# Second FFN: stores on GpSimd's queue, raw tokens loaded half a pass earlier, one operand's split moved, six staging tiles at the end

## The chip, the cores and the metric

One core of a Trainium2 chip runs the whole program as one launch. The metric is the device time of the launch in microseconds (us), the median of several runs. Before the change it is 1320.53 us over three runs (1319.96 to 1321.88).

## The reference

```python
attn_out = attention between x [8,8,512,64] and state [8,8,32,64], rows of x and of state concatenated
x = attn_out.transpose(0, 2, 1, 3).reshape(B * S, H * D)      # 4352 used rows x 512 (8 * (512 + 32))
x = ((x @ w1) * (x @ w2)) @ w3 @ w_out                          # first FFN, d_ff 1024
gate = 1.0 / (1.0 + np.exp(-(x @ w_gate)))                      # second FFN, d_ff 1536
return (gate * (x @ w_val) @ w_out2).astype(np.float32)
```

The change lies in the second FFN alone: gate, value, product and down projection for 34 blocks of 128 tokens, and the stores of its result.

## The kernel before

**Order of the whole.** Attention and the first FFN run first and leave their result `y` in DRAM (`y_d`). The second FFN starts at about 540 us in the profiled execution. Each matrix product there is cut as Strassen-Winograd does it (seven products of half-size blocks, `OPS`, `SEQ`, `DOWN`), and each operand is split into a high and a low part (`split`, `operand`, `part`), so that one product is three matmuls per 128 rows of the contraction.

**Loops.** The tokens are cut into five pairs of chunks, `blocks = [8, 8, 6, 6, 6]` (line 239), so a matmul streams n = 512 columns in the first two and 384 in the last three. For each chunk `c` there are three passes `g` over a third of the hidden columns (`steps`, line 1591). One pass is `gate_val(c, g, 0, between)`, 14 steps, and `gate_val(c, g, 1, ...)`, 14 steps; three steps into the first half `between` runs `down` of the pass before, 7 products of 2 steps. A step is 6 matmuls.

**The order of the work.** It is written out by hand. `begin` counts the steps (`clock["now"]`) and runs what is due; `later(k, cost, fn)` makes `fn` due `k` steps on; `fill` puts token work into steps where VectorE has credit. PE, ACT, DVE, POOL and SP each execute in the order in which instructions were emitted.

**Weights.** `Stream` (lines 1245 to 1264) holds 16 tiles `wt` (256 KB each, one per step of `gate_val`) and 4 tiles `wo` (512 KB each, one per product of `down`). A tile's next load is issued on SP's queue when the tile has been used. With four `wo` tiles, the load issued after product s is needed by product s + 4.

**Stores.** After the last pass of a chunk, `store` (line 1478) is due for each of its blocks every three steps: VectorE transposes the block in 32x32 pieces into one of three `sv` tiles, and two steps later `out_` issues four DMAs of 64 KB on SP's queue (line 1486). The three `sv` tiles also hold copies of partial sums in `evict` (lines 1530 and 1538). The last chunk is stored by `last_store` (line 1493): TensorE transposes a block into a PSUM bank, ACT or DVE copies it into an `sv` tile, and one DMA of 256 KB stores it, on SP's queue for even and ACT's for odd blocks. All six of its blocks follow the last product (lines 1576 to 1580). Two of these six blocks (32 and 33, the second and third in order) are rows of `state`: their destination has the dimensions 4 by 32 by 512, the others 128 by 512.

**Tokens.** `next_tokens(c + 1, at)` (line 1268) issues the four raw loads of the next chunk on SP's queue (`y_raw`, line 1117), and lists eight differences (`diff`) and fourteen splits (`part`). Each split has a step count after `half[i]`, the middle of a pass. The call is at the start of a chunk's last pass (lines 1616 to 1620).

**Operands of the down projection.** `operand(s, jj)` (line 1336): ACT copies the high part, one step later VectorE makes the low part. Operands 0 to 3 are put into the schedule by `have` (line 1358), operands 4 to 6 by `down` itself (line 1575), four products ahead.

Of the kernel before, what the change touches and what calls it, by code (L numbers as in the profile page):

```python
# [8 lines left out]
F32 = mybir.dt.float32  # L9
# [108 lines left out]
def tile_state_attention__then__gated_ffns(  # L118
# [19 lines left out]
    nc = tc.nc  # L138
    P = 128
    B, H, S, D = x.shape  # L140
    NS = state.shape[2]
    DM, DFF = w1.shape
# [6 lines left out]
    KM = DM // P  # L149
# [87 lines left out]
    NPAIR = 5  # L237
# [6 lines left out]
    NPASS = 3  # L244
# [18 lines left out]
    with tc.manual_schedule(engines={mybir.EngineType.PE}):  # L263

        at = tc.alloc_tile_pool(name="at", bufs=1, reuse_waits="tile")
# [830 lines left out]
        todo = []  # L1096
# [104 lines left out]
        ps2 = tc.alloc_tile_pool(name="ps2", bufs=1, space=PSUM, reuse_waits="tile")  # L1201
        tc.swap_default_side()
        c2 = tc.alloc_tile_pool(name="c2", bufs=1, reuse_waits="tile")
# [6 lines left out]
        clock = {"now": 0, "us": 0.0, "vector": 0.0, "load": 0.0}  # L1210
        due = {}
        tokens = []
        half = {}
        ready = {(0, o, kb) for o in range(7) for kb in range(2)}

        def later(k, cost, fn):
            due.setdefault(clock["now"] + k, []).append((cost, fn))
# [140 lines left out]
        def have(q, jj, cc, n):  # L1358

            cost = n / 840  # L1360
            if q == 0:
                if (jj, cc) == (1, 0):
                    for i in range(2):
                        later(2 + i, 0.0, lambda i=i: operand(0, i))
                        later(3 + i, cost, lambda i=i: first_sum(i, n))
                        later(5 + i, 0.0, lambda i=i: operand(1, i))
                return
            if cc:
                later(3, cost, lambda: minus(tv[jj], pv[1, jj, 1], tv[jj]))
                later(6, cost, lambda: minus(pv[0, jj, 1], pv[1, jj, 1], pv[0, jj, 1]))  # L1370
                if jj == 0:
                    for i in range(2):
                        later(4 + i, 0.0, lambda i=i: operand(2, i))
                        later(6 + i, 0.0, lambda i=i: operand(3, i))
            elif jj:
                for i in range(2):
                    later(5 + i, cost, lambda i=i: minus(tv[i], pv[1, i, 0], tv[i]))
# [100 lines left out]
        def store(c, cc, m):  # L1478
            t = c2.tile([P, 4, KM, 32], F32, name="sv", bufs=3)
            for d in range(KM):  # L1480
                nc.vector.transpose(out=t[:, :, d], in_=acc[d, cc][:, m * P : (m + 1) * P])

            def out_():
                dst = rows(c, cc, m)
                for i in range(4):
                    nc.sync.dma_start(
                        out=dst[:, :, i * P : (i + 1) * P],
                        in_=t[32 * i : 32 * i + 32].rearrange("t j d e -> t j (d e)"),
                    )

            later(2, 0.0, out_)

        def last_store(c, cc, m, i):
            pt = ps2.tile([P, DM], F32, tag="A", name="pot", bufs=2)
            for d in range(KM):
                nc.tensor.transpose(pt[:, d * P : (d + 1) * P], acc[d, cc][:, m * P : (m + 1) * P], unit)
            t = c2.tile([P, 4, KM, 32], F32, name="sv", bufs=3)
            copy("dve" if i % 2 else "act", t, pt.rearrange("p (c i d) -> p i c d", c=KM, i=4))
            blk = first[c] + (cc * blocks[c] // 2) + m
            if blk < B * SC:  # L1500
                b, r = order[blk // SC], blk % SC
                dst = out[b * ROWS : b * ROWS + S].rearrange("(p c) e -> c p e", c=SC)[r]
            else:
                b = 4 * (blk - B * SC)
                dst = out.rearrange("(b r) e -> b r e", b=B)[b : b + 4, S:]
            (nc.scalar if i % 2 else nc.sync).dma_start(out=dst, in_=t.rearrange("p i c d -> p (i c d)"))

        def down(c, g, tail=False):
            n = blocks[c] * P // 2
            banks = {}  # L1510

            def more(o, d, cc):
                nc.vector.tensor_tensor(out=acc[d, cc], in0=o, in1=acc[d, cc], op=ALU.add)  # L1513
                vector(n / 840)

            def also(v, d, cc):
                nc.vector.tensor_tensor(out=acc[d, cc], in0=v, in1=acc[d, cc], op=ALU.add)

            def new_acc(d, cc):
                acc[d, cc] = c2.tile([P, NB], F32, name=f"acc{d}{cc}")[:, :n]  # L1520
                return acc[d, cc]

            def evict(k, d, o):
                if k == 1:
                    if g == 0:
                        s = new_acc(d, 0)
                        copy("act", s, o)
                        later(1, n / 1600, lambda: nc.vector.tensor_copy(out=new_acc(2 + d, 0), in_=s))
                    else:
                        s = c2.tile([P, NB], F32, name="sv", bufs=3)[:, :n]  # L1530
                        copy("act", s, o)
                        later(1, n / 840, lambda: also(s, d, 0))
                        later(2, n / 840, lambda: also(s, 2 + d, 0))
                elif k == 5:
                    if g == 0:
                        copy("act", new_acc(2 + d, 1), o)
                    else:
                        s = c2.tile([P, NB], F32, name="sv", bufs=3)[:, :n]
                        copy("act", s, o)
                        later(2, n / 840, lambda: also(s, 2 + d, 1))  # L1540
                elif k == 6:
                    if g == 0:
                        copy("act", new_acc(d, 1), o)
                    else:
                        more(o, d, 1)
                else:
                    e = {3: (d, 1), 7: (2 + d, 1), 2: (d, 0), 4: (2 + d, 0)}[k]
                    more(o, *e)

            for s, k in enumerate(DOWN):  # L1550
                w = wos.next()
                for d in range(2):
                    begin(1.36 * n / 512)
                    if k in (1, 6, 2):
                        tag, bufs = ("B", 2) if k == 6 else ("o", 3)
                        banks[k, d] = ps2.tile([P, 512], F32, tag=tag, name=f"po{k}", bufs=bufs)[:, :n]
                    o = banks[{5: 1, 3: 1, 7: 6, 4: 6}.get(k, k), d]
                    for jj in range(2):
                        x = parts[s, jj]
                        for i, h in ((0, 0), (0, 1), (1, 0)):  # L1560
                            nc.tensor.matmul(  # L1561
                                o,
                                w[:, jj, i, d * P : (d + 1) * P],
                                x[h],
                                start=k in (1, 6, 2) and jj == 0 and i + h == 0,
                                stop=jj == 1 and i == 1,
                                skip_group_check=True,
                            )
                    fill()
                    evict(k, d, o)  # L1570
                wos.load()
                for jj in range(2):
                    del parts[s, jj]
                    if s + AHEAD < len(DOWN):
                        later(1 + jj, 0.0, lambda s=s, jj=jj: operand(s + AHEAD, jj))
            if g == NPASS - 1:
                todo = [(cc, m) for cc in (1, 0) for m in range(n // P)]
                for i, (cc, m) in enumerate(todo):
                    if tail:
                        last_store(c, cc, m, i)  # L1580
                    else:
                        later(2 + 3 * i, 1.0, lambda cc=cc, m=m: store(c, cc, m))

        names = [(f"p{q}{jj}{cc}", 1, NB) for q in range(2) for jj in range(2) for cc in range(2)]
        names += [(f"acc{d}{cc}", 1, NB) for d in range(KM) for cc in range(2)]
# [27 lines left out]
        }  # L1613
        with tc.manual_schedule(engines=ordered):
            for i, (c, g) in enumerate(steps):
                if g == NPASS - 1 and c + 1 < NPAIR:
                    def at(k, i=i):
                        return lambda: i in half and clock["now"] > half[i] + k

                    tokens += next_tokens(c + 1, at)  # L1620

                def between():
                    if i:
                        down(*steps[i - 1])

                gate_val(c, g, 0, between)
                half[i] = clock["now"]
                gate_val(c, g, 1, lambda: None)
            for _ in range(3):
                begin(0.0)  # L1630
            down(*steps[-1], tail=True)
            while due:
                begin(0.0)
# [31 lines left out]
```

## Time and profile before

| what | value |
|---|---|
| median of 3 runs | 1320.53 us (1319.96 to 1321.88) |
| the profiled execution's own time | 1318.98 us |
| its span, first to last instruction | 1317.2 us |
| PE busy | 1277.9 us (97%) |
| DVE busy | 950.4 us (72%) |
| ACT busy | 672.3 us (51%) |
| POOL busy | 24.9 us (2%) |
| DMA, mean rate over the span | 238 GB/s |

The span is what the trace covers; 1.8 us of the execution's own time lie around it. A busy PE counts the modelled ends of pipelined matmuls. In the chain of waits 84% of the span is PE and 6% DMA.

### The profile page before, as it was taken

The page shows a single profiled execution, that of the slowest core. Times are in us where ns is not written, and L with a number is a line of the kernel's source. Part 1 is how long each engine was busy: PE and PEld are TensorE (multiplying, and loading weights), DVE is VectorE, ACT ScalarE, POOL GpSimd, SP SyncE. Part 2 cuts the span into 40 slices and gives each one's busy share as a digit, 9 for nine tenths or more (in the row PEclk, how much of TensorE's full clock was granted, in tenths as well). Part 3 has the DMA queues.
Part 4 walks back from the last instruction along what each step waited for, and adds up shares of the span by engine and source line. Part 5 has one row for each costly group of instructions (what it writes and reads, how often), then busy time and mean ns, then how long its engine had stood idle before and what let it go on. Part 6 is the DMA issues. An engine that isn't in the chain of part 4 may idle for free.

```text
span 1317.2 us, 21517 instructions
## 1 busy us (share of the span) xinstructions
PE 1277.9 (97%) x7816; PEld 1103.7 (84%) x7816; DVE 950.4 (72%) x1839; ACT 672.3 (51%) x1307; POOL 24.9 (2%) x50
## 2 busy tenths in 40 slices
PE   7999999999999999999999999999899999999995
PEld 5487778878778789888888888889899999999994
DVE  6893889797797856265868857697377757786755
ACT  6993757667577555252354435344235334444432
POOL 0000000000000000000000000000000000000000
PEclk9999999999999999999999999999899999999998
DMA  9994597886987732676776967669788898889743
GB/s 309 351 274 137 184 306 243 297 295 252 330 268 286 281 114 73 206 252 203 251 200 192 253 195 237 201 188 269 246 264 251 245 288 287 253 237 294 245 146 96
DMA packets 181666, 312.86 MB, mean 238 GB/s; under 512 B 45368, under 2 KB 77624, under 8 KB 174648
## 3 DMA queue, kind: packets, MB, share of 16 engines
q1 hardware_dynamic: 169076, 264.43, 63.7%
q0 software_dynamic: 5760, 37.23, 7.8%
q10 hardware_dynamic: 6724, 9.83, 2.2%
q8 instruction: 62, 1.02, 0.3%
q14 instruction: 44, 0.36, 0.1%
HBM read 256.38 MB, written 55.05 MB: 236 GB/s over the span
## 4 chain that ended last, share of the span: by engine, by line
PE 84%; DMA 6%; DVE 5%; ACT 3%; issue 1%; SPq 0%; DVEq 0%; ACTq 0%
PE psA L1392 20%; PE po L1561 16%; PE psB L1392 10%; PE pab L225 9%; PE py L225 8%; PE psC L1392 5%; PE pab L228 4%; PE py L228 4%; DMA wo<-wod 3%; PE pwp L225 2%; PE psw L533 2%; DMA wq<-w12d 2%; PE pwp L228 1%; PE pxt L290 1%; DVE y L1123 1%; DMA out<-sv 1%
## 5 line engine op out<-in xcount | busy, mean ns | idle before, releaser
L1392 PE MATMUL psA<-y,wt 128*128 128x384 f32 (+1 forms) x1440 | 299.8, 356 | 0.0
L1392 PEld LDWEIGHTS psA<-y,wt 128*128 128x128 f32 x1440 | 258.9, 188 | 22.5
L1561 PE MATMUL po<-ph,wo 128*128 128x384 f32 (+1 forms) x1260 | 256.0, 362 | 14.6 <-DMA wo<-wod 11.2
L1561 PEld LDWEIGHTS po<-ph,wo 128*128 128x128 f32 x1260 | 229.5, 191 | 38.7 <-issue 8.3
L158 ACT ACTIVATE u<-psA 128x384 f32<-128x384 f32 (+1 forms) x120 | 64.0, 533 | 239.3 <-PE psA L1392 227.0
L1392 PE MATMUL psB<-y,wt 128*128 128x384 f32 (+1 forms) x720 | 159.5, 356 | 0.0
L1392 PEld LDWEIGHTS psB<-y,wt 128*128 128x128 f32 x720 | 130.0, 188 | 11.2
L225 PE MATMUL py<-u,wp 128*128 128x512 f32 (+1 forms) x576 | 131.8, 381 | 0.0
L225 PEld LDWEIGHTS py<-u,wp 128*128 128x128 f32 x576 | 102.8, 188 | 27.2 <-issue 7.9
L225 PE MATMUL pab<-aT,sw 128*128 128x512 f32 x448 | 122.1, 394 | 0.8 <-DVE aT L163 0.8
L1513 DVE TENSOR_TENSOR acc<-po,acc 128x384 f32<-128x384 f32 (+1 forms) x140 | 83.7, 607 | 37.3 <-PE po L1561 36.7
L225 PEld LDWEIGHTS pab<-aT,sw 128*128 128x128 f32 x448 | 82.6, 188 | 17.6 <-DVE aT L163 1.1
L1419 DVE TENSOR_TENSOR p<-psB,u 128x384 f32<-128x384 f32 (+1 forms) x60 | 36.6, 610 | 80.5 <-ACT u L158 72.9
L1421 ACT ACTIVATE p<-p 128x384 f32<-128x384 f32 (+1 forms) x90 | 50.6, 563 | 77.1 <-DVE p L1419 77.1
L1123 DVE TENSOR_TENSOR ph<-p,ph 128x384 fp32r<-128x384 f32 (+1 forms) x120 | 72.5, 605 | 10.4 <-ACT ph L158 10.4
L1392 PE MATMUL psC<-y,wt 128*128 128x384 f32 (+1 forms) x360 | 79.8, 356 | 0.0
L1392 PEld LDWEIGHTS psC<-y,wt 128*128 128x128 f32 x360 | 65.0, 188 | 5.6
L228 PE MATMUL pab<-aT,sw 128*128 128x512 f32 x224 | 69.1, 390 | 0.0
L228 PE MATMUL py<-u,wp 128*128 128x512 f32 (+1 forms) x288 | 67.7, 377 | 0.0
L158 ACT ACTIVATE ph<-p 128x384 fp32r<-128x384 f32 (+1 forms) x120 | 64.7, 561 | 0.0
L158 ACT ACTIVATE ph<-t 128x384 fp32r<-128x384 f32 (+1 forms) x90 | 49.6, 563 | 28.0 <-DVE t L1123 26.6
L1123 DVE TENSOR_TENSOR ph<-t,ph 128x384 fp32r<-128x384 f32 (+1 forms) x90 | 54.1, 604 | 10.8 <-ACT ph L158 10.8
(145 smaller groups left out, 1801.2 us busy)
## 6 DMA issues: line engine op xcount, KB each, us to landing
wt<-wd SPq DMA_DIRECT2D x420, 256.0 KB, 3.2
wo<-wod SPq DMA_DIRECT2D x105, 512.0 KB, 4.0
wq<-w12d SPq DMA_DIRECT2D x32, 1024.0 KB, 8.7
raw<-in_moe_w SPq DMA_DIRECT2D x32, 512.0 KB, 6.1
wd<-wstb POOLq DMA_DIRECT2D x12, 1024.0 KB, 5.4
raw<-in_moe_w_out SPq DMA_DIRECT2D x20, 512.0 KB, 5.6
wd<-wsta POOLq DMA_DIRECT2D x12, 768.0 KB, 4.2
xn<-in_x SPq DMA_DIRECT2D x56, 128.0 KB, 6.5
```

The costliest lines, as they stand in the source:

```text
L158: return nc.scalar.activation(out=o, in_=i, func=AF.Copy)
L225: nc.tensor.matmul(o, w[i], xx[k], start=begin and n == 0 and i + k == 0, stop=False)
L228: nc.tensor.matmul(o, w[1 - late], xx[late], start=False, stop=end and n == len(pairs) - 1)
L290: nc.tensor.transpose(pt[:, c * P : (c + 1) * P], xn[b][:, g, c].rearrange("p a d -> p (a d)"), ident,)
L533: nc.tensor.matmul(pts[k][NS * g : NS * g + NS, a * WQ : (a + 1) * WQ], stT[64 * k : 64 * k + 64, g, self.b * NS : (self.b + 1) * NS], w[6 ...
L1123: nc.vector.tensor_tensor(out=o, in0=x0, in1=x1, op=ALU.subtract)
L1392: nc.tensor.matmul(o, w[:, i, kb * P : (kb + 1) * P], xx[kb][h], start=start, stop=i == 1 and kb == 1, skip_group_check=True,)
L1419: nc.vector.tensor_tensor(out=t, in0=o, in1=kept[a, what], op=ALU.add)
L1421: later(2, 0.0, lambda: nc.scalar.activation(out=t, in_=t, func=AF.Sigmoid))
L1513: nc.vector.tensor_tensor(out=acc[d, cc], in0=o, in1=acc[d, cc], op=ALU.add)
L1561: nc.tensor.matmul(o, w[:, jj, i, d * P : (d + 1) * P], x[h], start=k in (1, 6, 2) and jj == 0 and i + h == 0, stop=jj == 1 and i == 1, sk ...
```

## The change

Operand 3 of the down projection is split three steps later. The stores of the first four chunks are issued by GpSimd's queue and not by SP's. In the last chunk the six stored blocks are staged in the six `yt` tiles (tag `m`) and not in the three `sv` tiles, every third PSUM bank is of tag `C`, and the three blocks of the second half are transposed and stored one product earlier (after product 2, the sixth of the seven, before product 4). The next chunk's tokens are begun in the middle of the second pass instead of at the start of the third; the step counts of their splits still refer to the middle of the third.

```diff
-                        later(6 + i, 0.0, lambda i=i: operand(3, i))
+                        later(9 + i, 0.0, lambda i=i: operand(3, i))
...
                 for i in range(4):
-                    nc.sync.dma_start(
+                    nc.gpsimd.dma_start(
                         out=dst[:, :, i * P : (i + 1) * P],
...
-            pt = ps2.tile([P, DM], F32, tag="A", name="pot", bufs=2)
+            tag, bufs = ("C", 1) if i % 3 == 2 else ("A", 2)
+            pt = ps2.tile([P, DM], F32, tag=tag, name="pot", bufs=bufs)
...
-            t = c2.tile([P, 4, KM, 32], F32, name="sv", bufs=3)
+            t = c2.tile([P, 4, KM, 32], F32, tag="m", name="yt", bufs=6)
...
-            if g == NPASS - 1:
-                todo = [(cc, m) for cc in (1, 0) for m in range(n // P)]
-                for i, (cc, m) in enumerate(todo):
-                    if tail:
-                        last_store(c, cc, m, i)
-                    else:
-                        later(2 + 3 * i, 1.0, lambda cc=cc, m=m: store(c, cc, m))
+                if tail and k in (2, 4):
+                    for m in range(n // P):
+                        last_store(c, int(k == 2), m, (k == 4) * n // P + m)
+            if g == NPASS - 1 and not tail:
+                for i in range(2 * n // P):
+                    cc, m = 1 - i // (n // P), i % (n // P)
+                    later(2 + 3 * i, 1.0, lambda cc=cc, m=m: store(c, cc, m))
...
-                if g == NPASS - 1 and c + 1 < NPAIR:
-                    def at(k, i=i):
-                        return lambda: i in half and clock["now"] > half[i] + k
-
-                    tokens += next_tokens(c + 1, at)
-
...
                 half[i] = clock["now"]
+                if g == NPASS - 2 and c + 1 < NPAIR:
+                    def at(k, i=i + 1):
+                        return lambda: i in half and clock["now"] > half[i] + k
+
+                    tokens += next_tokens(c + 1, at)
                 gate_val(c, g, 1, lambda: None)
```

## Rows read from the trace of the kernel before

**Rows 1.** Groups by line: engine, operation, shapes, count | busy us, mean ns | idle us, releasers.

```profile
L1561 PE MATMUL po<-ph,wo 128*128 128x384 f32 (+1 forms) x1260 | 256.0, 362 | 14.6 <-DMA wo<-wod 11.2 <-ACT sv L158 3.4
```

**Rows 2.** Timeline of PE: start, us, what, [idle before it, and its releaser].

```profile
929.94 9.30 PE L1561 MATMUL po<-ph,wo 128*128 128x384 f32 x36 [5.23 <-DMA wo<-wod]
...
979.01 8.07 PE L1561 MATMUL po<-ph,wo 128*128 128x384 f32 x36 [2.32 <-DMA wo<-wod]
...
1116.73 6.48 PE L1561 MATMUL po<-ph,wo 128*128 128x384 f32 x36 [1.44 <-DMA wo<-wod]
```

**Rows 3.** Chain of waits in order of time: start, us, what.

```profile
916.38 6.26 PE po L1561 x36
923.26 6.54 DMA wo<-wod
...
968.36 2.09 PE po L1561 x12
970.47 8.40 DMA wo<-wod
```

**Rows 4.** Timeline of SP's queue: start, us, issues.

```profile
905.39 1.37 SPq L1260 DMA_DIRECT2D wt<-wd  x3
907.17 1.76 SPq L1486 DMA_DIRECT2D out<-sv  x4
909.03 1.36 SPq L1260 DMA_DIRECT2D wt<-wd  x3
...
965.68 2.49 SPq L1117 DMA_DIRECT2D yf<-yd  x4
```

**Rows 5.** DMA issues by line: KB each, median us to landing.

```profile
wo<-wod SPq DMA_DIRECT2D x105, 512.0 KB, 4.0
```

**Rows 6.** Windows: us, busy of each engine, granted clock of PE, DMA share, GB/s.

```profile
930.00:939.00 9.00, 9.00 (x36) 9.00 (x37) 2.79 (x5) 0.00 (x0) 0.00 (x0) 0.66 0.48 152
...
953.00:965.00 12.00, 12.00 (x71) 12.00 (x70) 6.79 (x14) 5.22 (x12) 0.00 (x0) 1.00 0.80 251
...
972.00:980.00 8.00, 5.68 (x33) 5.39 (x33) 7.15 (x16) 2.79 (x7) 0.00 (x0) 1.00 1.05 385
980.00:990.00 10.00, 10.00 (x50) 10.00 (x49) 6.70 (x13) 0.98 (x2) 0.00 (x0) 0.83 0.58 167
```

**Rows 7.** DMA issues on POOL, from the views of lines 662 and 1089: ns min/median/max.

```profile
L662 POOL DMA_DIRECT2D w12d<-wq x4: 533/602/1096, 21.9 to 47.9; - x4
...
L1089 POOL DMA_DIRECT2D wd<-wsta x12: 531/531/540, 156.9 to 420.5; - x12
```

**Rows 8.** Timeline of ACT, DVE and PE from 1015 to 1022 us.

```profile
1017.86 0.93 ACT L158 ACTIVATE ph<-p 128x384 fp32r<-128x384 f32 x2
...
1019.22 1.34 PE L1561 MATMUL po<-ph,wo 128*128 128x384 f32 x6 [0.95 <-ACT sv L158]
...
1019.86 0.53 ACT L1421 ACTIVATE p<-p 128x384 f32<-128x384 f32 x1 [0.69 <-DVE p L1419]
```

**Rows 9.** Timeline of all engines from 1295 us to the end.

```profile
1296.09 1.94 DVE L1513 TENSOR_TENSOR acc<-po,acc 128x384 f32<-128x384 f32 x4
...
1299.21 1.03 PE L1496 MATMUL pot<-unit,acc 128*128 128x128 f32 x8
1299.41 0.56 DVE L1513 TENSOR_TENSOR acc<-po,acc 128x384 f32<-128x384 f32 x1 [0.48 <-PE po L1561]
...
1301.01 1.15 ACTq L1506 DMA_DIRECT2D out<-sv  x1
...
1312.90 0.69 DVE L159 COPY sv<-pot 128x512 f32<-128x512 f32 x1 [9.54 <-DMA out<-sv]
1313.63 0.35 ACTq L1506 DMA_DIRECT2D out<-sv  x1
```

**Rows 10.** Windows of half a us in the last stores (columns as in rows 6).

```profile
1301.50:1302.00 0.50, 0.19 (x2) 0.00 (x0) 0.00 (x0) 0.00 (x0) 0.00 (x0) 1.00 1.02 385
...
1307.50:1308.00 0.50, 0.00 (x0) 0.00 (x0) 0.00 (x0) 0.42 (x1) 0.00 (x0) 0.50 0.31 70
```

## The prediction

> **What bounds the kernel now.** I read the views from coarse to fine. The table of the profile shows PE busy for 97% of the span, so what can be had is PE's idle time and slow time, not the work of another engine. The groups by line say where PE idles in the second FFN: its down projection waits 11.2 us for `wo` tiles and 3.4 us for ACT's copies into `sv` [rows 1]. PE's timeline places the `wo` waits: five, the longest 5.23 us at 929.94, then 2.32 at 979.01 and 1.44 at 1116.73, the other two sharing what is left, 2.2 us [rows 1, 2]. All lie in chunks with n = 384.
>
> The chain of waits in order of time says that they have two causes [rows 3]. At 916.38 a `down` begins. Its first product is two steps, and 12 matmuls take 2.09 us, so the first new `wo` load is due at 918.47. It is issued at 923.26, 4.8 us late, and lands 6.5 us later. SP's queue shows why it is late: before it, three `wt` loads and four stores alternate, and one such group takes 909.03 - 905.39 = 3.64 us [rows 4], while PE needs three `wt` tiles every 3 x 1.045 = 3.13 us. Each stored block thus puts SP back by 0.5 us. At 970.47, in contrast, the load is issued on time (968.36 + 2.09) but takes 8.40 us to land where the median is 4.0 [rows 3, 5]: four raw loads of tokens were issued at 965.68, just in front of it [rows 4], and the DMA engines are full, at a share of 1.05 and 385 GB/s [rows 6]. The wait at 1116.73 is the same collision one chunk on; the two unshown ones follow stores, as the first does.
>
> Two stalls cost a second time: TensorE's granted clock is 0.66 in 930 to 939 and 0.83 in 980 to 990 [rows 6], the stretches behind them. Part of each runs at 1.2 instead of 2.4 GHz.
>
> Last comes the end. The final matmul is done at about 1299.2, the last store is issued at 1313.63, and the span ends at 1317.2 [rows 9]: 18 us in which PE does only transposes. DVE's last copy starts at 1312.90 after an idle 9.54 us: it waited for a staging tile that an earlier store still held.
>
> **The change part by part**, against the profiled execution (1318.98 us, 1.55 us below the median; gains are carried over to the median unchanged).
>
> *Stores on POOL's queue.* SP loses 112 issues. Between two blocks it is left with three `wt` loads, 1.4 us per 3.13 us [rows 4], so it waits for PE and the `wo` load goes out when due: 918.47 + the 6.54 us it took [rows 3] is 925.0, and product 4 needs it at 916.38 + 8.4 = 924.7. By the median, 4.0, it is well in time. So the waits after stores go: 11.2 - 2.32 - 1.44 = 7.4 us, and the slow clock at 930, 9 x (1 - 0.66) = 3.0 us. On POOL nothing else is queued in this phase. The 40 DMAs that it issues earlier take 0.53 to 1.10 us each [rows 7]; four at 0.53 are 2.1 us per block, inside 3.13. The store's bytes stay on the DMA engines, so I leave 1 us of new waiting for them. **Gain 9.4**, bounds 0 (the stores delay weights wherever they are issued) and 10.4.
>
> The Trainium skill speaks against this part: DMA: Bandwidth & Descriptors, Rules for kernel authors, says that spreading DMAs over issuing engines does not help, since all run on the same 16 DMA engines, and saves only issue time. By it the gain here would be 0 (the first rival below) if issue time were not the bound; that SP's groups take 3.64 us against 3.13 is the row that says it is.
>
> *Raw loads half a pass sooner.* The four loads (384 KB each at n = 384) now meet 14 + 3 steps, 17.8 us, of `wt` loads with 16 tiles ahead before the next `down`. Beside the 251 GB/s that PE eats (256 KB per 1.045 us), 385 GB/s leave 134, so 1.57 MB are made up for in 11.7 us. SP meets four more issues there, 2.5 us [rows 4], covered by the 16 tiles. So 2.32 + 1.44 us go, and 10 x (1 - 0.83) = 1.7 us of slow clock. **Gain 5.5**, bounds 0 and 5.5. The eight differences on DVE go along into the second half of the pass, where DVE has room (6.79 us busy of 12 in 953 to 965 [rows 6]; the eight are 4.5 us at 0.56), and raw and `yt` tiles are held longer, which nobody waits for; no gain and no cost.
>
> *Operand 3.* Its two ACT copies (0.93 us at 1017.86) stand before the copy into `sv` for which PE idles 0.95 us at 1019.22 [rows 8]; behind it, PE starts earlier. But the second `sv` copy stands behind a sigmoid at 1019.86 that waits for DVE, and that order stays: what is saved at the first wait is paid at the second. Its two low parts on DVE move behind four additions, to about the time when product 3 reads them. Forecast **0**; bounds: all 3.4 us of `sv` waits gained, or one DVE operation late, 0.56 us [rows 9], in each of 15 `down`, 8 us lost.
>
> *The end.* Twelve of the 24 transposes move before the last 12 matmuls: 1.03 us per 8 [rows 9], 1.55 us, only shifted. They need additions that DVE works off at 1296.09 to 1298.03, the second of them by about 1297.1, when product 2 ends: no wait, at most 0.5 us. The other twelve wait for the last addition (1299.41 + 0.56 is 0.8 us after the last matmul). With a staging tile for each block, the last issue is bounded by 1299.2 + 1.55 + 0.8 + 1.55 of transposes + two copies (0.69, 0.60) + ACT's own issue of up to 1.15 us in front of its copy [rows 9], 1305.5 instead of 1313.63: 8.1 us gained if the transfers keep up. They may not. Blocks 32 and 33 move at 70 GB/s and a share of 0.31 where a plain block moves at 385 and 1.02 [rows 10], as if on a quarter of the engines. From the second store's issue, 1301.01, to the landing that frees the last copy, 1312.90, are 11.9 us. In the new order that store can go at about 1298.7 (DVE's 1298.03 + a copy); + 11.9 + 0.7 for a sixth block at 385 GB/s + 2 of finishing is 1313.3, a gain of 3.9, and 3 if the late transposes cost what they can. I take 5.5, between the two, nearer the transfers: **gain 5.5**, bounds 3 and 8.
>
> Sum: 9.4 + 5.5 + 0 + 5.5 = 20.4. 1320.5 - 20.4 = **1300.1**; I say 1300.
>
> **Rivals.**
>
> *The DMA engines, not SP's issue, are what the stores fill.* Then loads are as late as before after stores, and only the raw loads' waits and the end go: 5.5 + 5.5 = 11, 1309.5. For it: shares near 1 around the waits [rows 6]. Against it: the 923.26 load was issued late, not only slow. Chance 0.17.
>
> *POOL is too slow, and the kernel gets slower.* The three `sv` tiles are the place: if four issues on POOL take longer than 3.13 us (0.78 each), each block puts POOL back, DVE's transposes wait for a tile, and every DVE operation behind them waits, then PE. At the slowest POOL issue on record, 1.10 [rows 7], 20 blocks at n = 384 lose 4.4 - 3.13 and 8 at n = 512 (3.13 x 512 / 384 = 4.17 us per three steps) 0.23: 27 us, against 20.4 gained: 1327. It decides from about 1.0 us per issue on. Against it: the median is 0.53, for DMAs of the same 128 rows. Chance 0.05. The Trainium skill, SBUF — State Buffer, section SBUF: two separate sides, names such a mechanism: descriptors of DMAs issued from GpSimd cannot be written while VectorE runs a copy in a two-port mode, and it gives some 3.1 us instead of 0.62. By that figure, on every issue, it would be some 250 us lost; no row of this trace shows it.
>
> *Operand 3 comes late in every `down`:* 8 us lost of 20.4, 1308. Chance 0.08.
>
> *The raw loads only move their collision* into the second half-pass and still leave `wo` late: 5.5 less, 1305.6. Chance 0.08.
>
> **How the numbers follow.** The forecast has the remaining 0.62, and its own bounds reach from 1320.5 - 10.4 - 5.5 - 3.4 - 8 = 1293 to about 1306. The range reaches over the faster rivals, 1293 to 1310. 0.2% (2.6 us) is about what a measurement of this kernel can tell from no change. All cases but POOL's lie 10 us or more below the time before; I leave 0.02 in between for two of them together. Faster 0.92, same 0.03, slower 0.05.
>
> **What would show it.** Stores on POOL's queue at about 0.5 us each and no `DMA wo` among PE's releasers after them; `wo` landings near 4 us after the third pass begins; a granted clock of 1.0 from 925 on; the `sv` waits still there, not larger; the last store issued near 1305 and the span ending 4 to 6 us after it. Wrong would be: `wo` loads issued on time but landing in 6 us or more (first rival), DVE's transposes waiting for stores (second), PE waiting for `ph` in product 3 (third).

## The result, and the profile after

The change makes the kernel faster by what was forecast: 21.0 us were gained where 20.4 had been summed up.

| what | before | after |
|---|---|---|
| median of 4 runs | 1320.24 us | 1299.26 us (1298.55 to 1300.80) |
| ratio | 1 | 0.9845, 95% interval 0.9826 to 0.9863 |
| the profiled execution's own time | 1318.98 us | 1299.36 us |
| its span | 1317.2 us | 1296.9 us |
| PE idle in the down projection | 14.6 us | 5.4 us |
| mean granted clock of TensorE | 0.990 | 0.997 |

The groups by line of the kernel after (columns as in [rows 1]; the down projection's line is now 1562) show where PE's time came from, and where the stores went:

```profile
L1562 PE MATMUL po<-ph,wo 128*128 128x384 f32 (+1 forms) x1260 | 251.6, 357 | 5.4 <-ACT sv L158 2.8
...
L1486 POOL DMA_DIRECT2D out<-sv x112 | 61.6, 550 | 599.9 <-DVE sv L1481 593.5
```

`DMA wo`, 11.2 us in [rows 1], is no longer among PE's releasers. The waits view of the kernel after (engine, what waits, for whom: us in total, times, longest) says what the 5.4 us are:

```profile
PE po L1562 <- ACT sv L158: 2.8, 5, 1.1
PE po L1562 <- DVE ph L1123: 2.3, 4, 0.8
```

The waits for `sv` are a little smaller than the 3.4 us before. The waits for `ph`, the parts of the split operands, are new; [rows 1] have none. The chain of waits in order of time, around the `down` that began at 916.38 in [rows 3], holds no DMA any more; its 84 matmuls run through:

```profile
915.26 2.08 PE psA L1392 x12
917.35 1.04 PE psC L1392 x6
918.38 14.56 PE po L1562 x84
```

SP's queue in the same stretch (columns as in [rows 4]) has no stores between the weights, and the first new `wo` load goes out at 920.50, which is 918.38 plus the two steps of the first product; it was 4.8 us late before:

```profile
890.34 28.40 SPq L1260 DMA_DIRECT2D wt<-wd  x28
920.50 12.84 SPq L1260 DMA_DIRECT2D wo<-wod  x7
```

In the windows that answer to [rows 6] (same columns) the granted clock is 1.00, behind the first store wait as behind the third pass; before, 0.66 and 0.83 were granted there, a part of the time at 1.2 instead of 2.4 GHz:

```profile
930.00:940.00 10.00, 10.00 (x59) 10.00 (x59) 3.25 (x7) 2.38 (x5) 0.00 (x0) 1.00 0.88 279
...
975.00:985.00 10.00, 10.00 (x60) 10.00 (x59) 3.45 (x7) 2.87 (x6) 0.00 (x0) 1.00 0.88 282
```

The end is shorter too. In the timeline of all engines of the kernel after, product 2 ends at 1283.31, where the transposes that were moved begin; before, it ended at 1297.13 (the transposes' start of 1299.21 [rows 9] less the 2.08 us of the last product):

```profile
1283.31 1.47 PE L1497 MATMUL pot<-unit,acc 128*128 128x128 f32 x12
...
1285.11 1.15 ACTq L1507 DMA_DIRECT2D out<-yt  x1
...
1287.52 1.20 PE L1497 MATMUL pot<-unit,acc 128*128 128x128 f32 x9 [0.32 <-DVE acc L1514]
...
1289.49 0.34 ACTq L1507 DMA_DIRECT2D out<-yt  x1
```

**Where the 20.3 us of the span went.** `wo` waits 11.2; slow clock 3.0 + 1.7 = 4.7 (the prediction's terms from [rows 6]); from the end of product 2 to the end of the span 1317.2 - 1297.13 = 20.1 before and 1296.9 - 1283.31 = 13.6 after, 6.5 less; `sv` waits 0.6 less; `ph` waits 2.3 more. That is 20.7.

### The profile page after: what moved, and what is told of

Read it like the earlier page. It is cut to its first block, busy times and chain, and to the rows that moved or that the text cites. A ratio compares the mean times of both kernels' runs of the same rounds, so it can differ in the third digit from the quotient of the medians.

```text
span 1296.9 us, 21521 instructions
## 1 busy us (share of the span) xinstructions
PE 1273.8 (98%) x7816; PEld 1100.1 (85%) x7816; DVE 951.6 (73%) x1839; ACT 668.8 (52%) x1307; POOL 86.7 (7%) x162
## 4 chain that ended last, share of the span: by engine, by line
PE 86%; DVE 8%; ACT 3%; DMA 1%; issue 1%; ACTq 0%; SPq 0%; DVEq 0%
PE psA L1392 20%; PE po L1562 16%; PE psB L1392 10%; PE pab L225 9%; PE py L225 9%; PE pab L228 5%; PE psC L1392 4%; PE py L228 4%; PE pwp L225 2%; PE psw L533 2%; DVE y L1123 1%; PE pwp L228 1%; PE pxt L290 1%; DVE p L1428 1%; DVE ph L1123 1%; DMA wq<-w12d 1%
## 5 line engine op out<-in xcount | busy, mean ns | idle before, releaser
L1562 PE MATMUL po<-ph,wo 128*128 128x384 f32 (+1 forms) x1260 | 251.6, 357 | 5.4 <-ACT sv L158 2.8
L1562 PEld LDWEIGHTS po<-ph,wo 128*128 128x128 f32 x1260 | 225.1, 188 | 29.3 <-ACT sv L158 6.0
L1392 PEld LDWEIGHTS psB<-y,wt 128*128 128x128 f32 x720 | 130.0, 188 | 11.2
L1486 POOL DMA_DIRECT2D out<-sv x112 | 61.6, 550 | 599.9 <-DVE sv L1481 593.5
## 6 DMA issues: line engine op xcount, KB each, us to landing
wt<-wd SPq DMA_DIRECT2D x420, 256.0 KB, 3.5
```

What stands on the lines that cost most here:

```text
L1392: nc.tensor.matmul(o, w[:, i, kb * P : (kb + 1) * P], xx[kb][h], start=start, stop=i == 1 and kb == 1, skip_group_check=True,)
L1486: nc.gpsimd.dma_start(out=dst[:, :, i * P : (i + 1) * P], in_=t[32 * i : 32 * i + 32].rearrange("t j d e -> t j (d e)"),)
L1562: nc.tensor.matmul(o, w[:, jj, i, d * P : (d + 1) * P], x[h], start=k in (1, 6, 2) and jj == 0 and i + h == 0, stop=jj == 1 and i == 1, sk ...
```

## The experiments

All medians come with the kernel before run on the same chip, and the gains below are differences of these medians. The first four kernels take the kernel before and make one part of the change alone.

### The parts alone

**Stores alone.** The edit is the one word of the diff:

```diff
-                    nc.sync.dma_start(
+                    nc.gpsimd.dma_start(
```

> Of the change only the stores on GpSimd's queue. If SP's issuing is what makes the wo loads late: the three wo waits that follow stores (7.4 us together) and the slow clock at 930 (3.0 us) go, the two behind the raw loads (2.3 and 1.4 us) stay, about 1310. If the DMA engines are what the stores fill, whoever issues them: the waits stay, about 1320. If the moved loads of tokens are needed for the first waits to go as well: about 1320.

Measured: 1306.82 us against 1318.99, ratio 0.9906 (0.9882 to 0.9930): 12.2 us. PE's timeline in this kernel has no wait at 930, and of the five `wo` waits two places are left, those that the prediction gave to the raw loads:

```profile
972.00 8.05 PE L1561 MATMUL po<-ph,wo 128*128 128x384 f32 x36 [2.14 <-DVE acc L1513]
```

```profile
1107.89 6.48 PE L1561 MATMUL po<-ph,wo 128*128 128x384 f32 x36 [1.27 <-DMA wo<-wod]
```

The same bytes go over the same DMA engines, from another queue, and the three waits behind stores are gone. So the first rival, that the engines are what the stores fill, falls. By the span 10.8 us were gained: PE's waits in `down` fell from 14.6 to 6.8, and the slow clock at 930 took 3.0 with it.

**Raw loads alone.** The edit is the last part of the diff in front: the call of `next_tokens` goes behind the first half of the second pass.

> Of the change only the raw loads half a pass sooner. If the raw loads alone cause the waits at 979 and 1117: those go with the slow clock at 980, 3.8 + 1.7 us, about 1315; the waits that follow stores stay. If the loads only move their collision: about 1320.

Measured: 1316.37 us, ratio 0.9980 (0.9963 to 0.9997): 2.6 us, and not 5.5. The two named waits are gone, but PE's timeline shows the three behind stores, and two of them are longer than before:

```profile
931.36 7.80 PE L1561 MATMUL po<-ph,wo 128*128 128x384 f32 x36 [5.04 <-DMA wo<-wod]
...
1068.10 6.51 PE L1561 MATMUL po<-ph,wo 128*128 128x384 f32 x36 [1.85 <-DMA wo<-wod]
...
1204.05 8.00 PE L1561 MATMUL po<-ph,wo 128*128 128x384 f32 x36 [2.32 <-DMA wo<-wod]
```

The last two shared 2.2 us before and take 4.2 here, and behind the last one a stretch is at half the clock (window, columns as in [rows 6]):

```profile
1204.00:1207.00 3.00, 2.96 (x9) 2.99 (x10) 0.56 (x1) 0.00 (x0) 0.00 (x0) 0.50 0.70 262
```

Whether the raw loads' move made these waits longer is not shown. In the two kernels below that move neither stores nor raw loads, the same three waits come to 8.7 and 9.0 us, with 7.4 before and 9.2 here; in the kernel with the end alone, the first of them is

```profile
931.63 8.96 PE L1562 MATMUL po<-ph,wo 128*128 128x384 f32 x36 [6.00 <-DMA wo<-wod]
```

So from one profiled execution to the next these waits differ by more than 1 us, and only the 2.32 at 1204 stands out of what the others have (0.80 to 1.23). The 2.6 us are what the part gave alone; the interval of the ratio reaches from 0.4 to 4.9 us and leaves out the 5.5.

**Operand 3 alone.**

```diff
-                        later(6 + i, 0.0, lambda i=i: operand(3, i))
+                        later(9 + i, 0.0, lambda i=i: operand(3, i))
```

> Of the change only operand 3 three steps later. If it is neutral: within 1 us of 1320, with PE waiting for ph in product 3 by as much as it waits less for sv. If the low parts come late: 2 to 3 us slower. If its ACT copies were the sv waits' cause: 3 us faster, about 1317.

Measured: 1319.22 us against 1318.99, ratio 1.0005 (0.9988 to 1.0021): nothing. Behind the nothing stand several terms. The waits view of this kernel:

```profile
PE po L1561 <- DMA wo<-wod: 10.4, 4, 5.1
PE po L1561 <- DVE ph L1123: 4.2, 5, 1.8
PE po L1561 <- ACT sv L158: 2.3, 3, 1.1
```

1.1 us of `sv` waits are gone and 4.2 us for `ph` have come. But the longest of these five stands where [rows 2] have the 2.32 us for `wo` at 979.01, in front of the same 36 matmuls:

```profile
981.22 8.05 PE L1561 MATMUL po<-ph,wo 128*128 128x384 f32 x36 [1.84 <-DVE ph L1123]
```

The raw loads are still in their old place here, so this wait can be the old one under another name. The other four, 2.3 us in 3 of the 15 `down`, are as after the whole change: two with n = 512 and the last one.

**The end alone.** Only `last_store` and the place where `down` calls it are changed.

> Of the change only the end: six yt tiles, the third PSUM bank, the first three blocks one product earlier. If the end stands by itself: 6.5 us less, about 1314, the span ending some 13.6 us after product 2 ends. If the transfers bind and the earlier issues do not help them: 3 us, about 1317.

Measured: 1313.86 us, ratio 0.9962 (0.9948 to 0.9976): 5.1 us. In PE's and ACT's timeline the last issue stands 6.2 us behind product 2, as after the whole change:

```profile
1299.53 1.47 PE L1497 MATMUL pot<-unit,acc 128*128 128x128 f32 x12
...
1305.70 0.34 ACTq L1507 DMA_DIRECT2D out<-yt  x1
```

The span ends at 1314.2, 8.5 us after that issue: the transfers set the end, not the issues. From the end of product 2 it takes 14.7 us (20.1 before, 13.6 expected). The four parts sum to 12.2 + 2.6 - 0.2 + 5.1 = 19.7; together they gave 21.0.

### Why stores held SP back

Is it the time that SP needs for the issues, their number, or their bytes? This kernel has the stores on POOL's queue, and per stored block SP issues four DMAs of 512 bytes each, out of the same tile into a scratch tensor, which nothing reads:

```diff
+                for i in range(4):
+                    nc.sync.dma_start(
+                        out=note[4 * (first[c] + cc * blocks[c] // 2 + m) + i :][:1],
+                        in_=t[32 * i : 32 * i + 1, 0].rearrange("t d e -> t (d e)"),
+                    )
```

> The kernel before with its stores on GpSimd's queue, and for each of them one DMA of 512 bytes on SP's queue in its old place (112 of them, 57 KB in all, into a scratch tensor). If SP's issues are what makes the weights late, whatever they carry: the waits for wo after stores come back, most of 7.4 us and of the 3.0 us of slow clock, about 1317. If the stores' bytes on SP's own rings are: it stays at 1307.

Measured: 1310.59 us against 1319.02, ratio 0.9936 (0.9912 to 0.9961), against 0.9906 (0.9882 to 0.9930) without the small DMAs. The time lies between the two that were expected, and the intervals overlap; the traces tell more. By waits, the first place is back (PE's timeline):

```profile
928.50 8.92 PE L1567 MATMUL po<-ph,wo 128*128 128x384 f32 x36 [3.49 <-DMA wo<-wod]
```

and SP's queue shows groups that are as long as before, although the four small issues are shorter, 1.1 us instead of the 1.76 of [rows 4]:

```profile
906.09 1.11 SPq L1492 DMA_DIRECT2D note<-sv  x4
907.30 1.91 SPq L1261 DMA_DIRECT2D wt<-wd  x3
909.95 1.13 SPq L1492 DMA_DIRECT2D note<-sv  x4
```

From one group to the next are 909.95 - 906.09 = 3.86 us, more than PE's 3.13; the eight groups from 888.64 to 919.09 take 3.81 us each, and before the change the eight from 888.33 to 920.29 take 4.00. What fills them is in the waits of SP's own queue from 889 to 921:

```profile
SPq L1261 <- DMA wt<-wd: 7.1, 12, 1.6
...
SPq L1492 <- DMA wt<-wd: 2.6, 7, 0.7
```

SP waits 9.7 us for earlier DMAs to land. Before the change the same view has 1.3 and 1.2 us for `wt` and 0.6 for stores, 3.1 in all; with the stores alone moved SP waits there for PE only. In the instructions of this program SP's DMAs signal eight semaphores in turn, and an issue waits for the DMA eight places earlier. So seven issues per group on one queue cost twice: their issue time, and a lookahead of eight DMAs of which four are stores or, here, 512 bytes each. With the real stores issue time weighs most, 1.37 + 1.76 = 3.13 us of a group's 3.64 [rows 4]. That is just what PE leaves, so it is the rest, waits for landings and gaps between issues, that puts SP behind. The bytes are not needed to make this queue late. The small DMAs do not bring everything back, though: the waits at 1071 and 1207 stay away, and 8.4 of the 12.2 us are still gained. What the real stores do beyond this, by their longer issues or by their bytes, no run here separates.

**Does it need POOL?** The best kernel of the section on improvements below, with its stores on ACT's queue instead of POOL's:

```diff
-                    nc.gpsimd.dma_start(
+                    nc.scalar.dma_start(
```

> The kernel of e8_both with the stores of the first four chunks on ACT's queue instead of GpSimd's. If all that matters for the weights is that the stores leave SP: PE waits for no wo tile, as on GpSimd's queue. If ACT has time for 1.8 us of issues per block: 1295.5. If its issues delay its copies: PE waits for sv and PSUM copies instead, up to 28 blocks of 1 us, about 1300 to 1320.

Measured: 1314.92 us against 1317.77, ratio 0.9980 (0.9965 to 0.9995), where the same kernel with POOL has 1295.51. No `wo` wait follows a store here either, but ACT is late with everything else; PE's waits and timeline show it in the gate and value products:

```profile
PE psA L1392 <- ACT s L158: 8.3, 6, 2.1
```

```profile
908.22 1.31 PE L1392 MATMUL psA<-y,wt 128*128 128x384 f32 x6 [2.10 <-ACT s L158]
```

Behind these waits there are also two stretches at half the clock: granted are 0.53 in 1047 to 1054 and 0.52 in 1187 to 1194, and 1.00 in both with POOL (window, columns as in [rows 6]):

```profile
1047.00:1054.00 7.00, 5.90 (x18) 5.90 (x19) 3.76 (x10) 3.42 (x8) 0.00 (x0) 0.53 0.68 183
```

So it is not enough that the stores leave SP; of the two engines tried in its place, only the one that nobody waits for, POOL, keeps the gain.

### Loads or VectorE behind the third pass

In the kernel with the stores alone, the wait at 972.00 was put down to an addition on VectorE and not to a `wo` tile, as the prediction had it of 979.01 [rows 2]. There the `wo` load's landing and an unbroken chain of VectorE, with one of the eight differences in it, end together, and the change moves loads and differences at once. This kernel moves the stores and the loads, and holds the differences back to the third pass:

```diff
-                return lambda: all(k in landed and clock["us"] >= landed[k] for k in need)
+                return lambda: c in third and all(k in landed and clock["us"] >= landed[k] for k in need)
...
+                if g == NPASS - 1:
+                    third.append(c + 1)
```

> The kernel before with the stores on POOL's queue (as e1_stores_only) and the four raw loads issued in the middle of the second pass, but the eight differences on VectorE held back until the third pass begins, where they were. Question: what ended PE's wait of 2.14 us at 972.00 in e1_stores_only, where the wo load's landing (issued 964.12, 7.8 us) and VectorE's unbroken chain (957.42 to 971.88, with one of the eight differences in it) end together. Theory A, the raw loads: the wo load lands in 4 to 5 us, and both waits, at about 972 and 1108, are gone; the time falls by some 2.6 us, as the raw loads moved with the differences gave, to about 1304. Theory B, VectorE's backlog: the wait at about 1108 goes (there the wo load alone was late), but PE still waits 1.5 us or more for VectorE at about 972; the time falls by 1 to 1.5 us, to about 1305.5. PE's rows around the third down of the chunks with n = 384 decide, the times differ by less than they can tell.

Measured: 1305.03 us against 1316.44, ratio 0.9909 (0.9887 to 0.9932), which is also no faster than with the stores alone (0.9906). The time does not tell the theories apart, PE's timeline does:

```profile
962.47 3.28 PE L1562 MATMUL po<-ph,wo 128*128 128x384 f32 x18
966.58 11.74 PE L1562 MATMUL po<-ph,wo 128*128 128x384 f32 x66 [0.83 <-ACT sv L158]
```

Both named waits are gone. VectorE's chain was no shorter: its fourth addition from `po`, the one named at 972.00, ran to 974.48 here (the timeline of DVE):

```profile
973.93 0.55 DVE L1514 TENSOR_TENSOR acc<-po,acc 128x384 f32<-128x384 f32 x1
```

That is 2.7 us after product 4 began (966.58 plus 30 matmuls of 0.174 us, 971.8), and PE did not wait for it. What did change is the load. The first `wo` issue of this `down` (DMA issues in a window around it: KB, us to landing), first with the stores alone moved, then with the raw loads moved too:

```profile
wo<-wod SPq DMA_DIRECT2D x1, 512.0 KB, 7.8
```

```profile
wo<-wod SPq DMA_DIRECT2D x1, 512.0 KB, 3.7
```

So it was the raw loads in front of it, as the prediction had it, and the releaser that the view named was the one that happened to end last. But the differences are not free. PE's waits for `sv` are these:

```profile
PE po L1562 <- ACT sv L158: 5.1, 8, 0.9
```

They were 3.4 us in 6 with the stores alone, and are 3.5 in 7 with loads and differences moved (the kernel with operand 3 back, below). With the tokens there when the third pass begins, differences run from 961.64 on, in front of the sums that ACT's `sv` copies wait for. By the spans of the two profiled executions 1306.4 - 1302.9 = 3.5 us were gained (1.8 by the medians, none by the ratios), 1.7 less waiting and the 1.7 of slow clock behind 972 (granted 0.81 and 0.85 in the two windows of 5 us from 970 on with the stores alone, 1.00 here). Moving the differences along is worth another 1.6 us of waits, 5.1 less 3.5.

### What can be bettered

**Operand 3 back** (the kernel after, with `later(6 + i, ...)`):

> The changed kernel with operand 3 back at six steps. If the shift is neutral, as alone: within 1 us of the changed kernel's 1299.3, PE's waits for ph (2.3 us) gone and those for sv as before the change (3.4 us). If the waits for ph are a plain loss: 2 us faster, about 1297. If the shift helps once the other waits are gone: 1 to 2 us slower.

Measured: 1298.31 us (1296.53 to 1298.66) against 1319.02, ratio 0.9843 (0.9819 to 0.9867), the same as after the change (0.9845) within the interval. The `ph` waits are gone and the `sv` waits back:

```profile
PE po L1562 <- ACT sv L158: 3.5, 7, 0.9
```

**The two odd blocks in four pieces** (the kernel after, blocks 32 and 33 of the last chunk as four DMAs of 32 rows each):

```diff
+            if blk < B * SC:
+                queue.dma_start(out=dst, in_=flat)
+            else:
+                for j in range(4):
+                    queue.dma_start(out=dst[j], in_=flat[32 * j : 32 * j + 32])
```

> The changed kernel with the last stores of blocks 32 and 33 as four DMAs of 32 rows each instead of one DMA of 4 by 32 rows. If that shape keeps them on a quarter of the engines and this sets the end: the last packets come some 2 to 3 us earlier, about 1297. If all engines are full in the end anyway, or the six more issues cost as much: within 1 us of 1299.3.

Measured: 1296.40 us (1295.25 to 1298.48), ratio 0.9833 (0.9809 to 0.9857). The windows of the last stores, first of the kernel after, then of this one (columns as in [rows 6]; the last two are the DMA share and GB/s):

```profile
1291.00:1293.00 2.00, 0.00 (x0) 0.00 (x0) 0.00 (x0) 0.00 (x0) 0.00 (x0) 0.74 0.97 285
1293.00:1295.00 2.00, 0.00 (x0) 0.00 (x0) 0.00 (x0) 0.00 (x0) 0.00 (x0) 0.50 0.32 120
```

```profile
1293.00:1295.00 2.00, 0.00 (x0) 0.00 (x0) 0.00 (x0) 0.00 (x0) 0.00 (x0) 0.77 0.89 316
1295.00:1297.00 2.00, 0.00 (x0) 0.00 (x0) 0.00 (x0) 0.00 (x0) 0.00 (x0) 0.50 0.00 0
```

Here the stores run on nearly all engines to their end, and from the end of product 2 (1285.98) to that of the span (1296.6) it takes 10.6 us instead of 13.6. The row with 0.89 is mostly the plain blocks. They land 2.1 to 3.1 us after their issue here; in the kernel after, the three issued behind the odd blocks take 5.2 to 6.2 us. While only the pieces of an odd block move, 64 KB each and issued 0.44 us apart, the share is 0.55:

```profile
1291.00:1292.00 1.00, 0.40 (x4) 0.15 (x2) 0.82 (x2) 0.31 (x1) 0.00 (x0) 1.00 0.55 131
```

So the two blocks of the shape 4 x 32 x 512 were what the end waited for, through their shape and not their size. By time the medians are 2.9 us apart, but the intervals of the two ratios overlap. The Trainium skill, DMA: Bandwidth & Descriptors, section Why a DMA increments its semaphore by 16 and not by 1, states how many engines a DMA gets: the largest number up to 16 that divides the slowest dimension of both sides, here 4 of 128 and 4. The trace agrees: a share of 0.31, near a quarter, with such a block in flight [rows 10], and 0.55, more than a quarter, with its pieces.

**Both** (operand 3 back, blocks in pieces):

> Both of the last changes to the changed kernel: operand 3 at six steps, and blocks 32 and 33 in four DMAs each. If both help: 4 us faster, about 1295. If neither does: 1299.3.

Measured: 1295.51 us (1293.33 to 1296.17), ratio 0.9822 (0.9798 to 0.9846). Every run is below every run of the kernel after, though the intervals of the ratios overlap.

**The last waits of PE.** With both, operand 3 two steps later and the first sigmoid of a pass one step later; and the sigmoid alone:

```diff
-                    later(2, 0.0, lambda: nc.scalar.activation(out=t, in_=t, func=AF.Sigmoid))
+                    later(2 + (jj == cc == 0), 0.0, lambda: nc.scalar.activation(out=t, in_=t, func=AF.Sigmoid))
```

> The kernel of e8_both with operand 3 at eight steps and the one sigmoid that ACT runs ahead of the second sv copy a step later. If the sv waits of PE (3.7 us) hang on these two alone: most of them go, about 1292.5, without waits for ph. If the low parts then come late instead, or DVE's additions hold sv: within 1 us of 1295.5.

> The kernel of e8_both with the sigmoid a step later, operand 3 as there at six steps. If the sigmoid holds the second sv copy and the operand's ACT copies the first: about half of the sv waits go, 1 to 2 us, about 1294. If nothing changes: 1295.5.

Measured: 1296.34 us, ratio 0.9839 (0.9820 to 0.9857), and 1295.11 us (1294.05 to 1295.83), ratio 0.9832 (0.9813 to 0.9850). Neither is told from the kernel with both. In the first the named waits of PE in `down` are 1.4 us instead of 3.7, but the groups by line, of the kernel with both and then of this one, show that `down` got no shorter:

```profile
L1567 PE MATMUL po<-ph,wo 128*128 128x384 f32 (+1 forms) x1260 | 251.2, 357 | 3.8 <-ACT sv L158 3.7
```

```profile
L1567 PE MATMUL po<-ph,wo 128*128 128x384 f32 (+1 forms) x1260 | 253.5, 358 | 2.5 <-DVE acc L1519 1.1 <-DVE ph L1123 0.3
```

Busy and idle time together are 255.0 and 256.0 us. The weight loads of the same matmuls (engine PEld) tell where the wait went:

```profile
L1567 PEld LDWEIGHTS po<-ph,wo 128*128 128x128 f32 x1260 | 225.1, 188 | 27.2 <-ACT sv L158 6.7 <-DVE acc L1519 0.6
```

```profile
L1567 PEld LDWEIGHTS po<-ph,wo 128*128 128x128 f32 x1260 | 224.8, 188 | 28.6 <-DVE acc L1519 6.0 <-DVE ph L1123 1.9 <-ACT sv L158 1.1
```

With ACT's copies earlier, the sums on VectorE are what the loads wait for, for almost as long; this is close to the second case of what was expected. With the sigmoid alone, `sv` waits are 2.7 us in 3, and busy and idle time 253.8 us, 1.2 less than with both; the times cannot show so little.

## Why the prediction was right, step by step

**Stores on POOL's queue (9.4 forecast).** Right: 12.2 by the medians of the part alone, with an interval from 9.2 (0.0070 of 1319) to 15.6, and 10.8 by its span. The forecast's own terms, 7.4 of waits and 3.0 of clock, are 10.4; the 1 us that was withheld for new waiting of loads did not occur. The 7.4 come from one execution; the same waits were 8.7 and 9.0 in the two other kernels that keep the stores and the raw loads where they were. The reason given, SP's groups of 3.64 us against 3.13, was right, but it was called issue time, and that is one half of the mechanism: a group's issues alone take 3.13 us, no more than PE leaves. In the kernel with the small DMAs they take 1.1 + 1.4 = 2.5 us, less than that, and the queue was still late, for waits on its own earlier DMAs.

**Against the Trainium skill's rule** that spreading DMAs over issuing engines does not help (DMA: Bandwidth & Descriptors, Rules for kernel authors): its own exception, issue time, was one part of the point here; for bandwidth no run tests it. Nothing in that rule speaks of a queue that is held up by the landing of its earlier DMAs, which the runs showed beside it.

**POOL's cost (0.53 us per issue forecast).** Measured on line 1486 of the kernel after (ns min/median/max, first and last start):

```profile
L1486 POOL DMA_DIRECT2D out<-sv x112: 548/548/572, 719.6 to 1175.6; - x112
```

No issue came near the 1.0 us at which the second rival decides, VectorE waited for no store in `sv`, and a landing took 3.9 us in the median. The figure of 3.1 us, which the Trainium skill, SBUF — State Buffer, section SBUF: two separate sides, gives for a DMA issued from GpSimd beside VectorE's copies, was not put to the test. VectorE's copies between SBUF tiles in this part of the kernel are ten (line 1529, 0.36 to 0.43 us each), and none of them ran during one of the 112 issues; beside them VectorE did additions and transposes.

**Raw loads (5.5 forecast).** Right in its mechanism: both waits went, and the slow clock behind them. The size is not shown in time. Alone the part gave 2.6; in the whole change 21.0 - 12.2 - 5.1 + 0.2 = 3.9 are left for it; 5.1 stand in the traces, the 2.1 and 1.3 us of waits left with the stores alone and 1.7 of clock. "No gain and no cost" for the differences held as they were moved: `sv` waits are 3.4 us before and 3.5 with loads and differences moved. What the prediction did not see is that they had to move: left in the third pass they cost 1.7 us in `sv` waits once the tokens are early.

**Operand 3 (0 forecast).** Right by time. The argument, saved at the first `sv` wait and paid at the second, is what happened in the `down` that it was read from. Before, the second wait behind the 0.95 us of [rows 8] was

```profile
1020.81 11.73 PE L1561 MATMUL po<-ph,wo 128*128 128x384 f32 x66 [0.25 <-ACT sv L158]
```

and after the change the first is gone and the second is

```profile
1010.88 11.71 PE L1562 MATMUL po<-ph,wo 128*128 128x384 f32 x66 [1.09 <-ACT sv L158]
```

The same holds one chunk on (0.95 and 0.27, then 1.09). What the forecast left at 0 is the rest: the last `down` loses its `sv` wait of 0.76 us and waits 0.3 and 0.6 for `ph`, and two `down` with n = 512 wait 0.8 and 0.6 for `ph`. The third rival, 8 us lost in every `down`, was right in place and wrong in frequency: 3 of 15. By the waits of PE the shift costs 1.7 us (5.4 against 3.7 with operand 3 back), which the times do not tell from 0.

**The end (5.5 forecast).** 5.1 by the part alone, 6.5 by the span of the whole change. The last issue was put at 1305.5 at the latest, 8.4 us after product 2; it came after 6.2 to 6.3, in part as ACT's own issue in front of its copy took 0.34 us and not 1.15. It made no difference, since the transfers were the limit, as chosen: the span ends 7.4 and 8.5 us after the last issue, not 4 to 6.

The sum came closer than its terms: the stores gave 2.8 more than forecast and the raw loads alone 2.9 less. That these errors cancel is luck, and so is a miss of only 0.6 us. The parts' 19.7 and the whole's 21.0 differ by 1.3, which these medians do not tell from 0.

## What to carry to other kernels

When a prefetched load is late, look first whether it was *issued* late or *landed* late: the two have different cures, and here both stood in the same row of waits. A queue that feeds PE does best with nothing but its feed: here even DMAs of 512 bytes made it late, and the stores were cheap only on the engine that nobody waits for. A store at the very end of a kernel should have a destination whose slowest dimension uses all DMA engines.

## What the runs showed of the hardware that was not expected

- In this program SP's issues wait for SP's own landings, eight DMAs back, through the semaphores that its DMAs signal in turn. Four DMAs of 512 bytes per group on SP, 1.1 us of issuing, made it wait 9.7 us for `wt` loads to land in 32 us, against 3.1 for all landings with the four real stores, and none without either.
- A 256 KB store with the outer dimension 4 moved at a DMA share of 0.31 (70 GB/s) and the same bytes in four pieces at 0.55 (131 GB/s); this shortened the end of the kernel by 3.0 us in the trace.
- The issue of the same 64 KB store took 548 ns in the median on POOL (548 to 572 in 112 issues), 430 on SP (315 to 1683, kernel before) and 342 on ACT (322 to 612, stores on ACT's queue). POOL's was the longest and the steadiest.
- A releaser named in a row can be the wrong one of two that end within 0.2 us: the wait of 2.14 us "for `acc`" at 972.00 vanished when the load behind it landed 4 us sooner, with the addition later than before.
